# The first scan of a Mamba-2 layer and the MLP behind it: y in four PSUM banks, and copies, a mask, an identity fold and a mix in other places

## The chip, the cores and the metric

The kernel runs on one NeuronCore of a Trainium2 chip. The metric is device time in microseconds of one execution, as a median over runs. A profile is one execution recorded by the hardware profiler. PE is TensorE (matmuls), DVE is VectorE, ACT is ScalarE, POOL is GpSimd, and SP is the engine whose queue issues nearly all transfers. SBUF is the memory that all engines work on, and PSUM holds the results of matmuls in eight banks per partition.

## The reference

Two operations stand one behind the other. The first is a state space scan ("mamba2_ssd") over 4 batches of 8 heads, 768 positions, 32 features per head and 16 states, in chunks of 32:

```
for c in chunks:
    cum = cumsum(log a);  L = exp(cum_i - cum_j) where i >= j
    y[c]  = ((C B^T) * L) x  +  (C state) * exp(cum)
    state = exp(sum log a) * state + sum_j exp(cum_last - cum_j) * B_j x_j
```

Its y, as 3072 tokens of 256 features, goes into `h = y @ w_in` (256 to 2048), `g = h * sigmoid(1.702 h)` and `g @ w_out` (2048 to 256). The arguments x, a, B and C are of type float32. The two weights come as float64 and are turned to float32 on the chip.

## The kernel before, in words

**Tiling.** The 3072 tokens are cut into 6 groups of 512. A group is two pairs of 128-token chunks, and a chunk has two sides of 64 positions. The first group differs from the others in how its scan is made; its two pairs have the numbers 0 and 1. The order of the instructions on every engine is the order in which the program writes them down (`in_order` at the end), so whatever stands behind a waiting instruction on the same engine waits too.

**The first group.** Its steps are written out by hand at L1145 to L1193:

- `differ_of` and `decay_exp` (L551, L572) make the decays L of pairs 0 and 1, on PE and ACT.
- `mask_first(0)` (L645, on POOL) and `mask_blocks(1)` (L654, on ACT) make CT, which is C with the heads of a row group masked, for pairs 0 and 1.
- `fields(0)` and `rounded(0)` (L192, L195, L208, on DVE) begin the conversion of the first piece of w_in. `ends_first` (L465, DVE) makes Be.
- `score` (L677, PE) makes C B^T of both pairs in one PSUM area "cb" of four banks. `since_first` (L509 on PE, L514 on ACT) makes the decays since the start. `weigh` (L688, DVE) multiplies L by the scores, one instruction for each pair.
- Between the two weighings, `fetch(1, held=True)` writes one column of a buffer with a DVE memset (L171). The transfer of piece 1 of w_in waits for this memset, and with it everything behind it in SP's queue: pieces 2 to 5, and `rows_a`.
- `drops` (L519, DVE) copies the decays that carry a state on. `gain` (L708, PE) makes the increments of the states, `parts_first` (L727, ACT) masks them, `since_start` (L662, POOL) makes CsT, `clamp(0)` (L203, L204, ACT) goes on with the weights, and `keep_first` (L732 scan, then L737 copies on DVE and POOL) makes the states S.
- `fold_ident(1, nc.gpsimd)` (L332, POOL) makes the second half of a tile of identities, which `decay` needs from pair 3 on. `table(AF.Silu)` (L282, ACT) loads the table of Silu.
- `finish` makes y: `intra` (L814) and `inter` (L802) on PE, and two copies (L840, ACT) into yT. y lies in one PSUM area of four banks that takes the place of "cb", so its first matmul waits until the second `weigh` has read the scores. `dense(1)` (L1141) puts a matmul of ones on PE, whose result nobody reads.
- `join(0)` (L219, L225, DVE) ends piece 0 of w_in.

**The first group's MLP.** `hidden(0, f)` for f = 0 to 15 (L869 on PE, L873 Silu on ACT) needs w_in's pieces: piece 0 for f = 0, 1; piece 1 for 2, 3; piece 2 for 4, 5; piece 3 for 6, 7; piece 4 for 8 to 11; piece 5 for 12 to 15. `narrow(i)` converts piece i between these steps. Its order on DVE is `rounded(i)`, then `fields(i + 1)`, then `join(i)`. So the end of a piece stands behind the first look at the next one, which waits for that one's transfer. The ring of four PSUM banks "ff" holds h. `project_all(0)` (L967) follows, with the scan of the second group and the last pieces (8, 9) of the weights between its steps. Then come two steps `hidden(1, ...)`, the decay, scores and states of the third group, and from there on a form of Strassen's algorithm (`first`, L925 and L935; `product`, L1030; `mix`, L893 to L895), which has 7 products in the place of 8.

`mix_y(1)` (L893 to L895, DVE) makes the sums of yT that the second group's Strassen products need. It stands at place 15 of `project_all(0)`, ahead of `decay(n + 1)` (L399, then `ends`, L458), whose result the matmuls of `gain(later)` (L708) wait for.

Of the kernel before, what the change touches and what calls it, by code (L numbers as in the profile page):

```python
# [11 lines left out]
AF = mybir.ActivationFunctionType  # L12
# [4 lines left out]
P = 128  # L17
# [18 lines left out]
def kernel(  # L36
# [161 lines left out]
    def clamp(i):  # L198


        e = power[i]
        z = e.bitcast(FP32)
        nc.scalar.activation(z, e, AF.Relu, scale=-8.0, bias=edge[:, 0:1])  # L203
        nc.scalar.activation(e, z, AF.Relu, scale=-1.0, bias=edge[:, 1:2])  # L204

    def rounded(i):

        nc.vector.scalar_tensor_tensor(out=mantissa[i].bitcast(FP32), in0=bits[i][0],  # L208
                                       scalar=2.0 ** -32, in1=mantissa[i],
                                       op0=ALU.mult, op1=ALU.add)  # L210
# [21 lines left out]
    def narrow(i):  # L232
        rounded(i)
        if i + 1 < len(PIECES):
            fields(i + 1)
        join(i)
# [43 lines left out]
    def table(f):  # L280

        nc.scalar.activation(early, early, f)  # L282
# [47 lines left out]
    def fold_ident(k, engine=nc.vector):  # L330

        engine.tensor_tensor(  # L332
            out=idents[:, k * NH:(k + 1) * NH],
            in0=ident[:, :H].unsqueeze(1).to_broadcast([P, NH, H]),
            in1=ident[:, H:].unsqueeze(1).to_broadcast([P, NH, H]), op=ALU.add)
# [57 lines left out]
    yT = {}  # L393

    def decay(p):

        L = ssd.tile([P, 2 * NH * H], FP32, tag="L", name=f"L{p}", bufs=3)
        Ls[p] = L.rearrange("p (k r q i) -> p k r q i", k=2, r=R, q=Q)
        nc.vector.tensor_tensor_scan(  # L399
            out=L, data0=ra[p].rearrange("p k e -> p (k e)"),  # L400
            data1=idents.rearrange("p h i -> p (h i)"), initial=0.0, op0=ALU.mult, op1=ALU.add)
        for k in range(2):
            ends(p, k)
# [112 lines left out]

    def drops():

        nc.vector.tensor_copy(  # L519
            drop[:, :, 1:], since[0][:, :CG].rearrange("p c (s i) -> p (c s) i", s=2)[:, 1:, H - 1].unsqueeze(  # L520
                1).to_broadcast([P, Q * D, 2 * CG - 1]))

# [51 lines left out]
    def turn(p):  # L574
        turn_only(p)
        since_start(p)

    def bank(name):
        return ps.tile([P, 4 * P], FP32, tag="ff", name=name)

    def area(name):
        return psa.tile([P, R, 4 * P], FP32, tag="cb", name=name)
# [66 lines left out]
    def mask_blocks(p):  # L649

        s = st[p]
        s["CT"] = ssd.tile([P, 2, Q, P], FP32, tag="CT", name=f"CT{p}")
        for q in range(Q):
            nc.scalar.activation(s["CT"][:, :, q], s["tp"], AF.Copy, scale=part[:, q:q + 1])  # L654

    def since_start(p, engine=nc.vector):

        b, c = divmod(2 * p, NC)
        s = st[p]
        tp = s["tp"]  # L660
        s["CsT"] = ssd.tile([P, 2, P], FP32, tag="CsT", name=f"CsT{p}", bufs=3)
        engine.tensor_tensor(out=s["CsT"], in0=tp, in1=since[b][:, c:c + 2], op=ALU.mult)  # L662
# [66 lines left out]
    def keep_first():  # L729

        flat_steps = steps.rearrange("p e m -> p (e m)")
        nc.vector.tensor_tensor_scan(  # L732
            out=flat_steps, data0=drop.rearrange("p e m -> p (e m)"), data1=flat_steps,
            initial=0.0, op0=ALU.mult, op1=ALU.add)
        for p, copy in zip(range(PG), (nc.vector.tensor_copy, nc.gpsimd.tensor_copy)):
            state[p] = ssd.tile([P, 4, Q * D], FP32, tag="S", name=f"S{p}", bufs=3)
            copy(state[p], steps.rearrange("p e m -> p m e")[:, 4 * p:4 * p + 4])  # L737

# [36 lines left out]
    def finish(pairs, steps=range(2)):  # L775


        g, first = divmod(pairs[0], PG)
        early = pairs[0] < PG
        if 0 in steps:  # L780
            begun_y[pairs[0]] = area(f"y{pairs[0]}")[:, :, :len(pairs) * 2 * H].rearrange(
                "p (s t) (k i) -> p s t k i", s=2, i=H), set()
        both, begun = begun_y[pairs[0]]
        y = [both[:, i] for i in range(2)]

        def begin(i, t, parts):
            new = not begun & {(i, t, q) for q in parts}
            begun.update((i, t, q) for q in parts)
            return new

        def inter(n, p, sides=range(2)):

            for k in range(2):
                for i in sides:
                    m = 2 * k + i
                    if (4 * p + m) % (2 * NC) == 0:
                        continue
                    old = state[p][:, m - 1] if m else state[p - 1][:, 3]
                    for r in range(R):
                        t = r // 2  # L800
                        rows, to = slice(32 * r, 32 * r + 32), Q * D * (r % 2)
                        nc.tensor.matmul(  # L802
                            out=y[i][to:to + Q * D, t, 2 * n + k], lhsT=old[rows],
                            rhs=st[p]["CsT"][rows, k, SIDES[i]],
                            start=begin(i, t, range(Q * (r % 2), Q * (r % 2) + Q)), stop=early,
                            tile_position=(32 * r, to), skip_group_check=True)

        def intra(n, p):
            L = Ls[p]
            for k in range(2):  # L810
                for h in range(NH):
                    t, q = divmod(h, HB)
                    for i, side in enumerate(SIDES):
                        nc.tensor.matmul(  # L814
                            out=y[i][D * q:D * q + D, t, 2 * n + k], lhsT=rx[p][side, k, h],
                            rhs=L[side, k, h // Q, h % Q],
                            start=begin(i, t, (q,)), stop=not early, tile_position=(H * i, D * q),
                            skip_group_check=True)

        cols = slice(2 * first * P, 2 * (first + len(pairs)) * P)  # L820

        if first == 0:
            yT[g] = ffn.tile([P, NK, TG], FP32, tag="yT", name=f"yT{g}")
        if early:
            for n, p in enumerate(pairs):
                intra(n, p)
            dense(1)
            for i in range(2):
                for n, p in enumerate(pairs):
                    inter(n, p, (i,))  # L830
        else:
            for step in steps:
                for n, p in enumerate(pairs):
                    (inter, intra)[step](n, p)
            if 1 not in steps:
                return
        for i in range(2):
            o = yT[g][:, :, cols].rearrange("p t (k s i) -> p s t k i", s=2, i=H)
            if early:
                nc.scalar.activation(o[:, :, i], both[:, :, i], AF.Copy)  # L840
            else:
                nc.scalar.activation(o[:, i], y[i], AF.Copy)  # L842
        for p in pairs:
            state.pop(p - 1, None)
            st.pop(p)
            Ls.pop(p)
# [50 lines left out]
    def mix_y(g):  # L897
        mixed_y[g] = ffn.tile([P, 4, HT], FP32, tag="my", name=f"my{g}", bufs=1)
        mix(mixed_y[g], yT[g].rearrange("p k (t e) -> p k t e", t=2))
# [237 lines left out]
    def dense(n):  # L1137
        if n:
            t = bank("dense")
        for i in range(n):  # L1140
            nc.tensor.matmul(out=t[:, :4 * H], lhsT=ones,  # L1141
                             rhs=ones[:, :H].unsqueeze(1).to_broadcast([P, 4, H]),
                             start=True, stop=True, skip_group_check=True)
# [14 lines left out]
    mask_first(0)  # L1158
    for r in range(R):
        decay_exp(1, r, ab[1, r])  # L1160
    mask_blocks(1)
    turn_back()
    fields(0)
    ends_first(0)
# [13 lines left out]
        since_start(p, nc.gpsimd)  # L1178
    clamp(0)
    keep_first()  # L1180
    fold_ident(1, nc.gpsimd)
    table(AF.Silu)
    dense(1)
    finish(range(PG))
    dense(1)
    join(0)
    fields(1)
    clamp(1)
    rounded(1)
    fields(2)  # L1190
    clamp(2)
# [4 lines left out]
    def at(places, i, *work):  # L1196
        places.setdefault(i, []).extend(work)
# [13 lines left out]
    for i, k, c in ((2, 1, 1), (3, 2, 2), (4, 4, 4), (5, 6, 7), (6, 9, 12), (7, 12, 15)):  # L1211
# [2 lines left out]
    at(in_hidden[0], 9, lambda: spread(PG + 1), lambda: spread_rows(1))  # L1214
    n, p = 2 * PG, 3 * PG
    pairs = PG, PG + 1
    at(in_project[0], 0, lambda: turn(PG), lambda: narrow(8))
    at(in_project[0], 1, lambda: clamp(9))
    at(in_project[0], 2, lambda: decay(PG + 1), lambda: clip_rows(1),
       lambda: decay_rows(1), lambda: turn(PG + 1))  # L1220
# [4 lines left out]
    at(in_project[0], 15, lambda: finish(pairs, (1,)))  # L1225
    at(in_project[0], 13, lambda: mix_in(1), lambda: mix_in(2), lambda: mix_in(3),
       lambda: turn_blocks(2), lambda: decay(n))
    at(in_project[0], 15, lambda: mix_y(1))
    at(in_project[0], 6, lambda: spread(n), lambda: load(n), lambda: load_blocks(n + 1),
       lambda: load(n + 1, "b"), lambda: spread(n + 1))  # L1230
    at(in_project[0], 9, lambda: load(n + 1, "x"))
# [2 lines left out]
    after = {}  # L1234

    later = n, n + 1
    at(after, "H0", lambda: decay(n + 1), lambda: since_start(n),
       lambda: since_start(n + 1), lambda: gain(later), lambda: score(later),
       lambda: keep_both(later), lambda: weigh(n), lambda: weigh(n + 1))
    at(after, "H1", lambda: turn_out(0, 0), lambda: turn_out(0, 1))  # L1240
# [185 lines left out]
```

## Time and profile before

| what | value |
|---|---|
| median of 3 runs | 352.71 us (352.11 to 353.42) |
| the profiled execution | 351.27 us, span of its instructions 349.3 us |
| PE busy | 341.4 us (98%), 3388 instructions |
| DVE busy | 255.8 us (73%) |
| ACT busy | 149.2 us (43%) |
| POOL busy | 14.5 us (4%) |
| granted TensorE clock | 0.999 |
| transfers | 25.92 MB, mean 74 GB/s |

Matmuls are recorded as passes: one float32 matmul has two. In the timeline a row gives the start, the time from its first start to its last end, engine, line, operation, tiles and count; brackets hold the idle time of the engine ahead of it and what ended it. In the list of waits a row gives the total, the number of times and the longest. In the chain of waits a row gives the start, the time and what the end of the execution hung on.

### The profile page before, as it was taken

How to read it: one execution, taken by the hardware profiler on the slowest of the kernel's cores; microseconds unless marked ns; L12 is line 12 of the kernel's file. 1: busy time of each engine (PE TensorE's matmuls, PEld its weight loads, DVE VectorE, ACT ScalarE, POOL GpSimd, SP SyncE). 2: the span in 40 equal slices, each digit the busy share in tenths (PEclk: the TensorE clock that was granted, in tenths of full speed). 3: DMA queues.
4: the chain of work that ended last, by engine and by line, in shares of the span. 5: the costliest groups of instructions: out<-in, count | busy, mean ns of one | idle time of the engine just before them, and what ended most of it. 6: DMA issues, size and time to landing. Idle time of an engine off the chain costs nothing.

```text
span 349.3 us, 8110 instructions
## 1 busy us (share of the span) xinstructions
PE 341.4 (98%) x3388; PEld 272.9 (78%) x3388; DVE 255.8 (73%) x481; ACT 149.2 (43%) x332; POOL 14.5 (4%) x42
## 2 busy tenths in 40 slices
PE   7889999999999999999999999999999999999996
PEld 6634444547888888888888888888888888899996
DVE  5999998999679998739996558788464654455463
ACT  5778584005354322743442544432554331554320
POOL 8310000100000100000000000000000000000000
PEclk9999999999999999999999999999999999999999
DMA  6698998433626200445603026300000300000301
GB/s 163 149 324 179 242 217 189 84 84 69 116 39 145 47 0 6 73 81 108 116 21 56 2 70 123 66 0 3 0 4 2 60 2 1 0 2 0 62 0 61
DMA packets 89980, 25.92 MB, mean 74 GB/s; under 512 B 73432, under 2 KB 87128, under 8 KB 89944
## 3 DMA queue, kind: packets, MB, share of 16 engines
q1 hardware_dynamic: 89112, 24.88, 33.0%
q10 hardware_dynamic: 832, 0.52, 0.5%
q8 instruction: 26, 0.43, 0.5%
q14 instruction: 10, 0.08, 0.1%
HBM read 22.15 MB, written 3.24 MB: 73 GB/s over the span
## 4 chain that ended last, share of the span: by engine, by line
PE 75%; DMA 9%; DVE 8%; SPq 5%; issue 2%; ACT 0%; ACTq 0%; DVEq 0%
PE acc L1030 28%; PE X L925 19%; PE Y L935 14%; PE acc L1037 7%; DMA a<-scratch 4%; DMA bits<-in_moe_w_in_dram 3%; PE cb L677 2%; PE y L814 2%; SPq L180 2%; SPq L124 1%; DVE L L399 1%; PE y L802 1%; PE h L869 1%; DVE p L219 1%; SPq L150 1%
## 5 line engine op out<-in xcount | busy, mean ns | idle before, releaser
L930 ACT ACTIVATE ac<-X 128x256 f32<-128x256 f32 x76 | 29.1, 383 | 78.7 <-PE X L925 78.2
L1030 PE MATMUL acc<-mg,mw 128*128 128x256 f32 x192 | 54.5, 379 | 0.0
L902 ACT ACTIVATE gT<-gT 128x512 f32<-128x512 f32 (+1 forms) x76 | 39.3, 519 | 33.5 <-DVE gT L1057 32.8
L1057 DVE TENSOR_TENSOR gT<-Y,ac 128x512 f32<-128x512 f32 x38 | 26.2, 689 | 36.1 <-PE Y L935 30.4
L925 PE MATMUL X<-my,mi 128*128 128x256 f32 x152 | 45.1, 379 | 0.0
L1057 DVE TENSOR_TENSOR gT<-Y,b 128x256 f32<-128x256 f32 x38 | 15.9, 420 | 34.8 <-PE Y L935 34.8
L1030 PEld LDWEIGHTS acc<-mg,mw 128*128 128x128 f32 x192 | 36.5, 190 | 5.0
L869 PE MATMUL h<-yT,w_in 128*128 128x512 f32 (+2 forms) x108 | 35.6, 485 | 1.2 <-DVE w_in L225 1.2
L1030 PE MATMUL acc<-gT,w_out 128*128 128x256 f32 x128 | 35.5, 379 | 0.0
L869 PEld LDWEIGHTS h<-yT,w_in 128*128 128x128 f32 x108 | 18.2, 190 | 17.4 <-issue 13.6
L925 PEld LDWEIGHTS X<-my,mi 128*128 128x128 f32 x152 | 28.0, 190 | 3.7
L967 PE MATMUL o<-gT,w_out 128*128 128x512 f32 x64 | 28.6, 597 | 0.0
L893 DVE TENSOR_TENSOR mg<-gT 128x512 f32<-128x512 f32 x40 | 27.3, 682 | 0.0
L1030 PEld LDWEIGHTS acc<-gT,w_out 128*128 128x128 f32 x128 | 24.2, 190 | 3.4 <-ACT yT L842 0.2
L930 ACT ACTIVATE b<-X 128x256 f32<-128x256 f32 x38 | 14.6, 384 | 20.3 <-PE X L925 19.8
L925 PE MATMUL X<-yT,w_in 128*128 128x256 f32 x76 | 23.2, 389 | 0.0
L935 PE MATMUL Y<-my,mi 128*128 128x256 f32 x76 | 22.7, 381 | 0.1
L935 PE MATMUL Y<-yT,w_in 128*128 128x256 f32 x76 | 22.7, 381 | 0.0
L935 PE MATMUL Y<-yT,mi 128*128 128x256 f32 x76 | 22.5, 379 | 0.0
L925 PE MATMUL X<-my,w_in 128*128 128x256 f32 x76 | 22.5, 379 | 0.0
L967 PEld LDWEIGHTS o<-gT,w_out 128*128 128x128 f32 x64 | 11.8, 190 | 13.2 <-issue 12.6
L399 DVE TENSOR_TENSOR_SCAN L<-a,idents 128x1024 f32<-128x1024 f32 x9 | 20.5, 2279 | 0.1
(153 smaller groups left out, 543.4 us busy)
## 6 DMA issues: line engine op xcount, KB each, us to landing
a<-scratch SPq DMA_DIRECT2D x18, 256.0 KB, 5.1
bits<-in_moe_w_out_dram SPq DMA_DIRECT2D x8, 512.0 KB, 5.4
x<-in_x_dram SPq DMA_DIRECT2D x24, 128.0 KB, 3.4
out_dram<-ob SPq DMA_DIRECT2D x40, 64.0 KB, 1.9
bits<-in_moe_w_in_dram SPq DMA_DIRECT2D x8, 256.0 KB, 4.5
bits<-in_moe_w_in_dram SPq DMA_DIRECT2D x4, 512.0 KB, 10.9
b<-in_B_dram SPq DMA_DIRECT2D x20, 64.0 KB, 2.8
af<-in_a_dram SPq DMA_DIRECT2D x3, 384.0 KB
```

The costliest lines, as they stand in the source:

```text
L180: nc.sync.dma_start(out=dst[k], in_=src[k])
L399: nc.vector.tensor_tensor_scan(out=L, data0=ra[p].rearrange("p k e -> p (k e)"), data1=idents.rearrange("p h i -> p (h i)"), initial=0.0, ...
L869: nc.tensor.matmul(out=h[:, cols], lhsT=w_in[:, f, k], rhs=yT[g][:, k, cols], start=(k == 0 and e == 0), stop=(k == NK - 1), skip_group_ch ...
L893: nc.vector.tensor_tensor(out=t[:, 0:2], in0=B[:, :, 1], in1=B[:, 0], op=ALU.subtract)
L902: nc.scalar.activation(o, i, AF.Silu, scale=GELU_SCALE)
L925: nc.tensor.matmul(out=s["X"], lhsT=lhsT, rhs=rhs, start=i == "1", stop=i == "4", skip_group_check=True)
L930: nc.scalar.activation(copy, s["X"], AF.Copy)
L935: nc.tensor.matmul(out=o, lhsT=lhsT, rhs=rhs, start=s.pop("new", False), stop=i != "5", skip_group_check=True)
L967: nc.tensor.matmul(out=o[c], lhsT=w_out[:, c, f], rhs=gT[g, f // 2][:, f % 2], start=(f == 0), stop=(f == NF - 1), skip_group_check=True)
L1030: nc.tensor.matmul(out=acc[g][0][i][:, cols], lhsT=w, rhs=h[:, cols], start=(j == 0 and k == 0 and (i, 0) in begins), stop=(j == NF // 2 - ...
L1037: nc.tensor.matmul(out=o[k] if type(o) is list else o[:, cols], lhsT=h[:, cols], rhs=w, start=(j == 0 and (i, k) in begins), stop=(j == NF ...
L1057: nc.vector.tensor_tensor(out=o, in0=v, in1=w, op=ALU.add)
```

## The change

- y of the first group lies in four banks of the ring "ff" (one for each half of the tokens' features, t, and each side, i), and no longer in the area that held the scores. The matmuls of `inter` are put in order of t. After those of one t, two ACT copies of 128x256 evict its two banks. Before, two ACT copies of 128x512 followed after all of them.
- `drops` runs on ACT in the place of DVE. The second copy of `keep_first` runs on ACT in the place of POOL.
- The mask of pair 1 is one POOL operation (`mask_first(1)`) in the place of two ACT operations.
- `dense(1)` ahead of y becomes `dense(2)`; the two other dense matmuls, inside `finish` and behind it, are gone.
- `fold_ident(1)` goes from POOL to DVE, from ahead of y to place 0 of `project_all(0)`, between `rounded(8)` and `fields(9)`.
- `table(AF.Silu)` goes from ahead of y to behind `clamp(1)`.
- `mix_y(1)` goes from place 15 of `project_all(0)` to behind `decay(n + 1)`.

```diff
     def drops():
-        nc.vector.tensor_copy(
+        nc.scalar.copy(
             drop[:, :, 1:], ...
     def keep_first():
...
-        for p, copy in zip(range(PG), (nc.vector.tensor_copy, nc.gpsimd.tensor_copy)):
+        for p, copy in zip(range(PG), (nc.vector.tensor_copy, nc.scalar.copy)):
...
     def finish(pairs, steps=range(2)):
...
+            if early:
+                y = [bank(f"y0_{i}")[:, :2 * P].rearrange("p (k i) -> p k i", i=H) for i in range(4)]
+                begun_y[0] = [[y[2 * t + i] for t in range(NK)] for i in range(2)], set()
...
-            dense(1)
-            for i in range(2):
+            for t in range(NK):
                 for n, p in enumerate(pairs):
-                    inter(n, p, (i,))
+                    inter(n, p, (t,))
+                for i in range(2):
+                    nc.scalar.activation(
+                        yT[g][:, t, cols].rearrange("p (k s i) -> p s k i", s=2, i=H)[:, i], y[i][t],
+                        AF.Copy)
...
-    mask_blocks(1)
+    mask_first(1)
...
-    fold_ident(1, nc.gpsimd)
-    table(AF.Silu)
-    dense(1)
+    dense(2)
     finish(range(PG))
-    dense(1)
+    dense(0)
     join(0)
     fields(1)
     clamp(1)
+    table(AF.Silu)
     rounded(1)
...
-    at(in_project[0], 0, lambda: turn(PG), lambda: narrow(8))
+    at(in_project[0], 0, lambda: turn(PG), lambda: rounded(8), lambda: fold_ident(1),
+       lambda: fields(9), lambda: join(8))
...
-    at(in_project[0], 15, lambda: mix_y(1))
...
-    at(after, "H0", lambda: decay(n + 1), lambda: since_start(n),
+    at(after, "H0", lambda: decay(n + 1), lambda: mix_y(1), lambda: since_start(n),
```

More of the change, by code (lines that the diff above doesn't have):

```diff
@@ L780, in finish @@
         if 0 in steps:
[L781 to L784, printed above, removed]
+            if early:
+                y = [bank(f"y0_{i}")[:, :2 * P].rearrange("p (k i) -> p k i", i=H) for i in range(4)]
+                begun_y[0] = [[y[2 * t + i] for t in range(NK)] for i in range(2)], set()
+            else:
+                both = area(f"y{pairs[0]}")[:, :, :len(pairs) * 2 * H].rearrange(
+                    "p (s t) (k i) -> p s t k i", s=2, i=H)
+                begun_y[pairs[0]] = [[both[:, i, t] for t in range(NK)] for i in range(2)] + [both], set()
+        y, begun = begun_y[pairs[0]]
         def begin(i, t, parts):
@@ L789, in begin, with inter @@
             return new
-        def inter(n, p, sides=range(2)):
+        def inter(n, p, ts=range(2)):
             for k in range(2):
-                for i in sides:
+                for i in range(2):
                     m = 2 * k + i
@@ L800, in inter @@
                         t = r // 2
+                        if t not in ts:
+                            continue
                         rows, to = slice(32 * r, 32 * r + 32), Q * D * (r % 2)
                         nc.tensor.matmul(
-                            out=y[i][to:to + Q * D, t, 2 * n + k], lhsT=old[rows],
+                            out=y[i][t][to:to + Q * D, 2 * n + k], lhsT=old[rows],
                             rhs=st[p]["CsT"][rows, k, SIDES[i]],
@@ L814, in intra @@
                         nc.tensor.matmul(
-                            out=y[i][D * q:D * q + D, t, 2 * n + k], lhsT=rx[p][side, k, h],
+                            out=y[i][t][D * q:D * q + D, 2 * n + k], lhsT=rx[p][side, k, h],
                             rhs=L[side, k, h // Q, h % Q],
@@ L826, in finish @@
                 intra(n, p)
-            dense(1)
-            for i in range(2):
+            for t in range(NK):
                 for n, p in enumerate(pairs):
-                    inter(n, p, (i,))
+                    inter(n, p, (t,))
+                for i in range(2):
+                    nc.scalar.activation(
+                        yT[g][:, t, cols].rearrange("p (k s i) -> p s k i", s=2, i=H)[:, i], y[i][t],
+                        AF.Copy)
         else:
@@ L836, in finish @@
                 return
[L837 to L842, printed above, removed]
+            for i in range(2):
+                nc.scalar.activation(
+                    yT[g][:, :, cols].rearrange("p t (k s i) -> p s t k i", s=2, i=H)[:, i], y[2][:, i],
+                    AF.Copy)
         for p in pairs:
```

## The prediction

> **What bounds the kernel now.** I read the list of PE's waits first, since PE is busy for 98% of the span. PE waited seven times in all, and never after 86.2 us; these are the waits that the change comes near:
>
> ```profile
> PE y L814 <- DVE L L688: 1.2, 1, 1.2
> PE h L869 <- DVE w_in L225: 1.2, 2, 0.9
> PE A L708 <- DVE Be L458: 0.3, 1, 0.3
> PE y L802 <- DVE S L737: 0.3, 1, 0.3
> ```
>
> Behind 86.2 us a microsecond counts only if PE gets its work earlier or later. So what matters is when PE passes two points: the waits for w_in (0.88 us at 18.97 and 0.32 us at 33.26) and the 0.28 us at 86.20. PE's timeline shows the first two:
>
> ```profile
> 18.97 13.97 PE L869 MATMUL h<-yT,w_in 128*128 128x512 f32 x32 [0.88 <-DVE w_in L225]
> 33.26 3.67 PE L869 MATMUL h<-yT,w_in 128*128 128x512 f32 x8 [0.32 <-DVE w_in L225]
> ```
>
> The 32 passes are f = 0 to 7, 1.745 us each. At 33.26 f = 8 waits for w_in's piece 4. The chain of waits, read from 10 to 34 us, says what made that late:
>
> ```profile
> 10.61 0.71 PE cb L677 x32
> 11.34 1.24 DVE L L688 x2
> 12.60 0.37 SPq L180
> ...
> 18.29 11.01 DMA bits<-in_moe_w_in_dram
> ...
> 29.42 0.69 DVE p L192
> 30.11 0.60 DVE m L195
> 30.72 1.15 DVE p L219
> ```
>
> The reader sees a stream of transfers that starts at 12.60, as soon as the memset L171 (12.51) lets it, and whose last part, piece 5, lands at 29.30. DVE waits for it 0.30 us, and `join(4)` stands behind that look at piece 5: it ends at 33.12, and PE starts at 33.26. This time hangs on the **start of the stream**, not on y. The memset follows the first `weigh` (11.34), which waits for the second half of the scores.
>
> **The change, part by part.** Every sum is against the profiled execution: 351.27 us with a span of 349.3; the median of the runs shown is 352.71, so 1.44 us are added to come to it.
>
> *The head up to f = 0.* y no longer waits for the second `weigh` (1.2 us at 13.86), the drops leave DVE (0.69), the second state copy leaves POOL (0.86) and the fold leaves POOL. By itself: the second `weigh` ends at 13.71, scan 1.23, state copy 0.39, so S at 15.4 (before 16.09 and 16.59). `join(0)` takes 0.71 + 0.69 as L219 and L225 do at 20.81 and 21.55, and ends at 16.8 (before 18.82). `inter` of one t is half of 1.15, so t = 0 is done at 16.1. Two evictions of 128x256 take 0.66 (as the two of L514), so yT's first half stands at 16.85. f = 0 then begins near 17.0 in place of 18.97: **2 us earlier**. The ACT copies are not in the trace: the drops cost from 0.36 (ACT's 128x256) to 0.69 (DVE's own), the state copy from 0.36 to 0.86 (POOL's own); I take ACT's row for 512 elements, 0.58, and 0.4. The drops fit between the since rows (end 11.30) and the wait for A (12.04), and the state copy runs beside DVE's. The table load and its little activation (1.28 + 0.20) go behind `clamp(1)`. Behind them stand `clamp(2)` and the first Silu, which have over a microsecond. None of the moved steps issues a transfer, and SP's order is the same.
>
> But f = 2 needs piece 1, whose `join(1)` stands behind `fields(2)`, and piece 2's second half lands at 19.6 (issued at 14.31, 5.3 later). From that look to the end of `join(1)` took 2.1 us (20.14 to 22.24). So f = 2 begins at 21.8, not 20.5, and f = 8 would be wanted at 21.8 + 6 x 1.745 = 32.3. It still gets its weights at 33.1. **So the 2 us are worth nothing:** PE waits 1.3 us at f = 2 and 0.9 at f = 8. If that wait at f = 8 weren't there, the whole 2 us would be gained.
>
> *`mix_y(1)` behind `decay(n + 1)`.* The three mixes (82.01 to 83.53) leave the place ahead of the scan L399 (83.53) and L458, which end at 86.16. They would end at 84.8. PE gets there at 85.9, so the 0.28 us go. What is late next: `my` at 86.3, and PE reads it at 92.2. **-0.28 us.**
>
> *The fold on DVE* costs 0.68 (L332 at 3.13) at 54.2, where DVE idles 0.96 us for piece 9's transfer (55.19). Nothing; without that cover 0.68 on DVE, still off PE's path. *Dense:* one matmul fewer (0.70), in PE's idle time: nothing.
>
> *The mask of pair 1 on POOL* is the one that touches the stream. PE's rows end at 10.54, so the scores begin there in any case, if POOL is done. The risk lies with what runs beside it:
>
> ```profile
> 7.78 1.03 POOL L645 TENSOR_TENSOR CT<-Ct,part 128x512 f32<-128x512 f32 x1
> 8.50 0.59 DVE L192 TENSOR_SCALAR p<-bits 128x512 uint32<-128x512 uint32 x1 [0.22 <-DMA bits<-in_moe_w_in_dram]
> 9.02 0.41 DVE L195 TENSOR_SCALAR m<-bits 128x512 uint32<-128x512 uint32 x1
> 10.14 0.68 DVE L208 SCALAR_TENSOR_TENSOR m<-bits,m 128x512 f32<-128x512 uint32 x1
> 11.11 1.42 POOL L662 TENSOR_TENSOR CsT<-Ct,since 128x256 f32<-128x256 f32 x2 [2.30 <-ACT since L514]
> 15.73 0.86 POOL L737 COPY S<-steps 128x256 f32<-128x256 f32 x1 [3.21 <-DVE steps L732]
> 16.01 1.14 DVE L219 SCALAR_TENSOR_TENSOR p<-bits,p 128x512 uint32<-128x512 uint32 x1
> 16.56 1.71 POOL L332 TENSOR_TENSOR idents<-ident 128x512 f32<-128x512 f32 x1
> 17.18 1.64 DVE L225 SCALAR_TENSOR_TENSOR w_in<-m,p 128x512 f32<-128x512 f32 x1
> ```
>
> The last four rows show DVE and POOL taking turns. L219 ends 0.56 us after the POOL copy's end (16.59), the fold ends 1.12 after L219's end (17.15), L225 ends 0.55 after the fold's end (18.27); alone, L219 and L225 take 0.7. L192 too ends 0.28 after POOL's mask (8.81). So each seems to wait for the other's whole instruction, and the one that waited first goes first. With a second mask waiting from 8.81: L192 ends at 9.09 as before, the mask runs 1.03 to 1.12 and ends at 10.12 to 10.21 (in time for 10.54), L195 ends 0.28 later, at 10.40 to 10.49 in place of 9.43. Be (PSUM input) and the start of L208 follow at the spacing they have now (0.71 after L195's end), so L208 comes at 11.11 to 11.20. There it meets POOL's CsT, which comes at 11.11. If CsT is first, L208 waits for 0.71 (half of 1.42) until 11.82 and ends 0.55 later, at 12.4: the first `weigh` starts at 12.35 in place of 11.34, **1.0 us later**. If L208 is first, it ends at 11.8 and the delay is 0.45. If they take no such turns here, DVE has 0.52 us of idle time ahead of L688, and the delay is 0. A gain is excluded by PE's rows, which hold the scores at 10.54. I take 1.0, since the fold's row and the mask's own both put L208 behind CsT. The stream, f = 8 and all that PE does behind it shift by as much; so does the head, which stays about 1 us ahead.
>
> [...]
>
> Sum: +1.0 - 0.28 = **+0.7 us**: 352.0 for the profiled execution, 353.4 for the median.
>
> **The rivals.** (1) *L208 goes ahead of CsT:* +0.45 - 0.28 = +0.2, so 352.9. For it: the two come within 0.1 us. (2) *No delay of the stream:* -0.28, so 352.4. For it: DVE's 0.52 us of slack; against it: L219 and L225. (3) *The head's 2 us come through:* -2.0 - 0.28, so 350.4. That needs piece 5 to land 2 us earlier; nothing issues it earlier. Against it: the memset L171 stands behind the same `weigh` as before. (4) *Slower: TensorE's clock falls in the new waits.* The first matmuls (L437, 192 columns in 0.33 us each) ran at half the rate of L869 (512 in 0.44) for 3 us. PE's longest idle time so far, 1.2 us at 12.66, cost no such thing; the wait at f = 2 would be 1.3 and that at f = 8 1.0. If anything over 1.2 us brought the half rate back for 3.3 us behind f = 8, it would cost 1.65: +2.35, so 355.1. Against it: the granted clock is 9 in every slice.
>
> **How the numbers follow.** Chances: forecast 0.45, (1) 0.25, (2) 0.18, (3) 0.05, (4) 0.05, and 0.02 for others. The first three hold 0.88 and lie from 352.4 to 353.4. The three runs shown lie up to 0.7 us from their median, so the range is 352.0 to 354.1. What a measurement of this kernel can tell from no change is about 0.5%, 1.76 us. All three are within it: faster 0.05 (rival 3), same 0.89, slower 0.06 (rival 4 and 0.01).
>
> **What would show it.** Right: L195 beside a POOL mask taking over 1 us; the memset L171 at 13.5 (13.0 for rival 1, 12.5 for rival 2); f = 0 at about 18.0 and PE waits at f = 2 and f = 8 for DVE's w_in; f = 8 at 34.3 (33.7, 33.3); no wait of L708 for L458. Wrong: f = 8 before 33.0, or a new wait of PE behind 34 us.

## The result and the profile after

| what | before | after |
|---|---|---|
| median, first comparison (22 runs of each) | 352.17 us (350.9 to 354.01) | 351.82 us (350.39 to 353.46) |
| median, second comparison (29 and 12 runs) | 351.67 us | 350.55 us |
| the profiled execution, and its span | 351.27 us, 349.3 us | 352.58 us, 350.7 us |

The ratio of after to before is 0.9992 (95% interval 0.9977 to 1.0008) in the first comparison and 0.9964 (0.9947 to 0.998) in the second. The second interval lies below 1, the first does not. So the change is worth between nothing and half a per cent; by the prediction's bound of 0.5% it is **no change that can be told**. The prediction said this of the sign, with 0.89. Its time, 353.4 us, was 1.6 us too high, and 351.82 lies 0.18 us below its range. All ratios here are of fast executions; one slow execution each of e7 (714.64 us), e8 (360.61) and e9 (1460.66) is left out of them.

The profiled execution of after is one of its slower ones (352.58 against a median of 351.82), that of before one of its faster ones (351.27 against 352.17). The two traces must therefore not be set against each other by their spans. They were read wait by wait, and a second profile of after was taken (e9 below). First the waits of PE after, with the total, the number and the longest:

```profile
PE y L820 <- issue: 1.6, 2, 0.9
PE h L876 <- DVE w_in L225: 1.5, 1, 1.5
...
PE b L624 <- ACT L L572: 0.5, 1, 0.5
```

The wait of y for the second `weigh` (1.2) is gone, that of y for the states (0.3) and that of A for Be (0.3) too. The two waits for w_in (1.2 together) have become one of 1.5. New is a wait of y "for issue": no semaphore that the profile shows ended it. PE's timeline of after has both waits of that kind, and the one for w_in:

```profile
13.81 1.57 PE L820 MATMUL y<-L,x 64*32 64x64 f32 x95
16.05 0.48 PE L820 MATMUL y<-L,x 64*32 64x64 f32 x33 [0.67 <-issue]
16.45 1.67 PE L808 MATMUL y<-CsT,S 32*64 32x64 f32 x56
18.12 3.70 PE L876 MATMUL h<-yT,w_in 128*128 128x512 f32 x8
23.33 12.91 PE L876 MATMUL h<-yT,w_in 128*128 128x512 f32 x29 [1.51 <-DVE w_in L225]
...
79.17 1.10 PE L820 MATMUL y<-L,x 64*32 64x64 f32 x88
81.16 0.65 PE L820 MATMUL y<-L,x 64*32 64x64 f32 x40 [0.89 <-issue]
```

The 128 passes of one y fall apart in 95 + 33 and in 88 + 40, in the middle of a run in which nothing changes. f = 0 starts at 18.12 (18.97 before), f = 2 at 23.33, and f = 8 at 33.86 without a wait of its own (23.33 plus 6 x 1.745 makes 33.80).

The part on which the forecast turned, DVE and POOL around the second mask, in the timelines of these two engines:

```profile
7.93 2.03 POOL L645 TENSOR_TENSOR CT<-Ct,part 128x512 f32<-128x512 f32 x2
8.63 1.62 DVE L192 TENSOR_SCALAR p<-bits 128x512 uint32<-128x512 uint32 x1
10.17 0.42 DVE L195 TENSOR_SCALAR m<-bits 128x512 uint32<-128x512 uint32 x1
11.17 0.68 DVE L208 SCALAR_TENSOR_TENSOR m<-bits,m 128x512 f32<-128x512 uint32 x1
11.90 1.44 POOL L662 TENSOR_TENSOR CsT<-Ct,since 128x256 f32<-128x256 f32 x2 [1.94 <-ACT since L514]
12.14 2.36 DVE L688 TENSOR_TENSOR L<-L,cb 128x1024 f32<-128x1024 f32 x2 [0.30 <-PE cb L677]
13.31 0.06 DVE L171 MEMSET bits<- 128x1 uint32 x1
```

The two masks run back to back on POOL (7.93 to 9.96), and one L192 waits for both: it takes 1.62 us (0.59 before) and ends at 10.25, 0.29 us behind the second. DVE makes up the rest of it in its idle time: L208 ends at 11.85, and the first `weigh` still waits 0.30 us, for PE's scores. The memset comes at 13.31, near the forecast's 13.5, but for another reason: PE was late. Its matmuls at L551 began at 6.41 us, against 5.62 in the trace of before, and the row ahead of that, in PE's timelines of after and then of before, shows why:

```profile
4.57 1.91 PE L545 MATMUL ab<-below,identb 128*128 128x256 bf16 x8
```

```profile
4.31 1.04 PE L545 MATMUL ab<-below,identb 128*128 128x256 bf16 x8
```

The same eight matmuls took 1.91 us in one execution and 1.04 in the other. Nothing of the change stands ahead of them. The trace's own record of the granted clock tells the two apart: it begins with the full rate at 4.04 us in before and at 6.52 us in after, and the slow passes end near there.

### The profile page after: what moved, and what is told of

Same layout as the page of the kernel before. It is cut to its first block, busy times and chain, and to the rows that moved or that the text cites. A ratio compares the mean times of both kernels' runs of the same rounds, so it can differ in the third digit from the quotient of the medians.

```text
span 350.7 us, 8109 instructions
## 1 busy us (share of the span) xinstructions
PE 342.9 (98%) x3386; PEld 273.8 (78%) x3386; DVE 255.7 (73%) x481; ACT 149.9 (43%) x334; POOL 13.1 (4%) x41
## 4 chain that ended last, share of the span: by engine, by line
PE 94%; DVE 2%; DMA 2%; SPq 1%; issue 0%; ACT 0%; DVEq 0%
PE acc L1037 28%; PE X L932 19%; PE Y L942 14%; PE h L876 9%; PE o L974 8%; PE acc L1044 7%; PE y L820 2%; PE cb L677 2%; DMA bits<-in_moe_w_in_dram 2%; PE y L808 1%; PE A L708 1%; PE busy L437 1%; PE ab L551 1%; SPq L180 1%; PE ab L545 0%
## 5 line engine op out<-in xcount | busy, mean ns | idle before, releaser
L937 ACT ACTIVATE b<-X 128x256 f32<-128x256 f32 x38 | 14.6, 384 | 20.2 <-PE X L932 19.7
L974 PEld LDWEIGHTS o<-gT,w_out 128*128 128x128 f32 x64 | 11.8, 190 | 13.2 <-issue 12.8
```

Source lines behind the costliest of these rows:

```text
L937: nc.scalar.activation(copy, s["X"], AF.Copy)
L974: nc.tensor.matmul(out=o[c], lhsT=w_out[:, c, f], rhs=gT[g, f // 2][:, f % 2], start=(f == 0), stop=(f == NF - 1), skip_group_check=True)
```

## The experiments

The first eight were planned on two questions: whether the waits "for issue" come from the few PE instructions by which the change shifts y, and what each other part of the change is worth. The last four settle the size of the mask's cost and the nature of those waits. All of them compute the whole reference. Times are medians; each ratio is against the kernel before in the same comparison, with its 95% interval. It isn't the quotient of the two medians: in e5 they lie on opposite sides of no change.

| run | from | time us (before beside it) | ratio |
|---|---|---|---|
| e1_pad | after | 351.45 (351.47) | 0.9995 (0.9975 to 1.0014) |
| e2_before_less_dense | before | 351.75 (351.47) | 1.0001 (0.9979 to 1.0022) |
| e3_mask_on_act | after | 350.76 (351.47) | 0.9993 (0.9968 to 1.0017) |
| e4_stream_first | after | 350.77 (351.47) | 0.9983 (0.9965 to 1.0001) |
| e5_old_y | after | 351.54 (351.27) | 0.9981 (0.9962 to 1.0) |
| e6_before_stream_first | before | 351.02 (351.27) | 0.999 (0.9972 to 1.0008) |
| e7_pads | after | 358.42 (351.27) | 1.0176 (1.0138 to 1.0214) |
| e8_together | after | 358.19 (351.27) | 1.0167 (1.0127 to 1.0207) |
| e9_after_again | after | 350.55 (351.67) | 0.9964 (0.9947 to 0.998) |
| e10_before_mask_alone | before | 351.78 (351.67) | 1.0007 (0.9983 to 1.0032) |
| e11_pads17 | after | 354.8 (351.67) | 1.0097 (1.006 to 1.0135) |
| e12_mask_and_stream | after | 350.41 (351.67) | 0.9973 (0.9952 to 0.9994) |

**e1_pad.** After, with one small matmul more ahead of the scan (two passes), so that everything behind the first y stands on PE where it stood before the change (the first y itself stands four passes further on than before, two of them by the second dense matmul).

```diff
-            pads(0, busy)
+            pads(1, busy)
```

> The changed kernel with one tiny matmul more (32x32, two passes, 4 instructions on PE) ahead of the masks, so that all of PE's later instructions stand 4 places further on in its instruction stream, about as in the kernel before. Theory 1 (instructions): in the profile of the changed kernel PE stops twice inside a run of small matmuls of y with nothing to wait for but 'issue' (0.67 us at 16.05, 0.89 us at 81.16), because the next block of its instructions was asked for too late; one dense matmul less moved the place at which it is asked for. Then the stall at 81 goes and the time falls by 0.9 to 1.2 us. Theory 2 (the stalls are an accident of the one execution): no change, within 0.3 us, and stalls of this kind stand in this profile too.

The wait in the second group's y stays, 0.72 us at 80.95, one of 0.23 us stands in the first y, and the time is that of before. So the few instructions that the change takes away aren't the cause.

**e2_before_less_dense.** Before, without the dense matmul ahead of y, so that all behind the first y is shifted as in after.

```diff
     table(AF.Silu)
-    dense(1)
     finish(range(PG))
```

> The kernel before without the one dense matmul ahead of y (4 instructions on PE fewer). Theory 1 (instructions): a stall 'issue' of about 0.9 us appears in the second group's y (near 80 us), and the time rises by 0.9 to 1.2 us. Theory 2 (accident): same time within 0.3 us, no such stall; the dense matmul lies in PE's idle time.

A wait appears (0.42 us at 81.33), smaller than after's. Together with e1 the picture was unclear: the waits come with the shift and without it.

**e3_mask_on_act.** After, with the mask of pair 1 back on ACT.

```diff
-    mask_first(1)
+    mask_blocks(1)
```

> The changed kernel with the mask of pair 1 back on ACT. Theory A (turns of DVE and POOL): L192 takes about 0.6 us in the place of 1.62, the first weighing and the memset that lets the stream go come earlier by up to 0.5 us (less if PE's scores are late in that execution), and the time falls by 0.3 to 0.5 us. Theory B (the scores on PE set the memset in any case): memset at the end of the scores plus 1.3 us as now, same time within 0.2 us.

L192 takes 0.43 us again, but the memset comes at 13.23, 1.28 us behind the end of the scores (11.95). With the mask on POOL it was 1.28 behind them too (12.03 and 13.31). So the mask's place costs the stream nothing in these executions. No y wait for issue is in this profile, though the program stands on PE as after's does.

**e4_stream_first.** After, with the memset, the fetches of pieces 1 to 5 and `rows_a` ahead of the scores.

```diff
-    score(range(PG), since_first)
-    weigh(0)
     fetch(1, held=True)
...
     rows_a(az, (nc.sync,))
+    score(range(PG), since_first)
+    weigh(0)
     weigh(1)
```

> The changed kernel with the memset and the transfers of pieces 1 to 5 and of a put ahead of the scores and of both weighings, so that the stream starts about 1.3 us earlier (near 12.0 by the last profile, or when DVE is through with rounded(0)). Theory S (the stream's start sets f = 2 and f = 8): PE's wait at f = 2 falls from 1.5 us to near 0 and the time falls by 1.2 to 1.5 us. Theory H (what the scan's first half takes on PE, DVE and ACT sets them): no gain, within 0.3 us. If the transfers of x and of the first blocks are disturbed by the stream, the time rises.

The memset comes at 11.76, and the wait at f = 2 goes. But y now waits 1.31 us, at the same 95th pass as in after. PE's timeline of this run:

```profile
14.01 1.54 PE L820 MATMUL y<-L,x 64*32 64x64 f32 x95
16.86 0.48 PE L820 MATMUL y<-L,x 64*32 64x64 f32 x33 [1.31 <-issue]
```

f = 0 starts at 18.94 and f = 8 at 33.27. What the earlier stream gives, the longer wait takes.

**e5_old_y.** After, with the old `finish`: y in the area of the scores, evicted at its end, and three single dense matmuls. It keeps the moved copies, mask, fold and mix.

> The changed kernel with y as it was: one PSUM area that waits for the second weighing, evicted by sides at the end, and the three single dense matmuls. All other edits stay. Theory S (the stream of w_in's pieces decides): f = 0 starts some 0.5 to 1.5 us later than in the changed kernel (18.1), and f = 2 and f = 8 stand where they stood against the memset L171 (10.0 and 20.5 us behind it), so the time is the same within 0.3 us. Theory Y (the four banks bring what the change brings): 0.5 to 1.5 us slower.

f = 0 comes 6.45 us behind the end of the scores; before it is 7.74, after 6.09, and in e9 5.85. So the copies, the fold and the table load made some 1.3 us of the head, and the halves of y some 0.5. f = 8 waits 1.52 us for w_in and starts at 33.63.

**e6_before_stream_first.** The edit of e4, made in before.

> The kernel before with the memset and the transfers of pieces 1 to 5 ahead of the scores and weighings. Theory S: before, f = 8 waited only 0.32 us for the stream, and f = 0 waits for join(0), which the stream does not touch, so the gain is 0.3 us at most, against up to 1 us for the same edit in the changed kernel. Theory H (the stream's start matters by itself): the same gain as in the changed kernel with this edit.

Again the memset is early (11.54), and again y waits for issue, here behind its 97th pass, for 1.20 us at 16.97. The waits belong to no version.

**e7_pads** and **e8_together.** After with 24 small matmuls and 2 dense ones at the start in the place of 5 dense ones, which moves all that follows by 42 passes; e8 has the edits of e3 and e4 as well.

```diff
-    keep_busy(5, 0)
+    keep_busy(2, 24)
```

> The changed kernel with 24 tiny matmuls in the place of three of the five first dense ones: PE is as busy there for about as long, but all later PE instructions stand 84 places further on in its instruction stream, and so the places where a new block of instructions is asked for and where it is needed. Theory I (PE stalls named 'issue' are waits for a block of instructions that was asked for behind a burst of transfers): no stall in the first y (it was 0.67 us) and none in the second group's y near 81 us (0.42 to 0.89 in three of six profiles), since the blocks are asked for about 84 instructions earlier in the same work; time 0 to 1 us less. Theory N (accident): stalls of this kind at the same places again, same time.

> The changed kernel with the stream first, the mask of pair 1 on ACT, and the 24 tiny matmuls. Theory S and I: f = 0 at about 17.5, no wait or a short one at f = 2, f = 8 at 32 to 32.5 in the place of 33.3 to 33.9, and no 'issue' stall at 81 us; time 0.8 to 1.5 us less than the changed kernel. If the stream was not what decided, the same time within 0.3 us.

Both lost 7 us, which no theory had foreseen. The list of PE's waits in e7, and its timeline:

```profile
PE y L820 <- issue: 3.6, 3, 1.7
PE y L808 <- issue: 3.3, 1, 3.3
```

```profile
13.61 0.98 PE L820 MATMUL y<-L,x 64*32 64x64 f32 x53
15.16 0.99 PE L820 MATMUL y<-L,x 64*32 64x64 f32 x75 [0.56 <-issue]
16.08 1.56 PE L808 MATMUL y<-CsT,S 32*64 32x64 f32 x52
20.98 0.47 PE L808 MATMUL y<-CsT,S 32*64 32x64 f32 x4 [3.34 <-issue]
```

The waits sum to 7.0 us (0.56, 3.34, 1.71 and 1.35), 5.4 more than after's waits for issue. With 2.3 us of half clock rate (below), 1.5 less at f = 2 and 0.4 less ahead of L551, that makes 5.8, and the spans of the two profiles differ by 5.7. The places explain the waits: counted from the start of the program they stand behind passes 349, 476, 2382 and 2892. After's and e1's stand behind 349 and 854, those of e4, e6, e9 and e12 behind 349, those of e2 and e10 in the second group behind 855. The count is the same whatever stands there, y's 53rd pass or its 95th. The distances are 127 (476 less 349), 505 (about 4 x 126), 1906 (about 15 x 127) and 510 (4 x 127.5). A pass has two PE instructions, a weight load and a matmul (the page of after counts 3386 of each), so there is such a place at every 256 instructions, a few semaphore instructions among them. The page's list of queues has one for instructions, and the transfers of e7 between 18.5 and 19.7 us have one entry of it; columns are packets, MB and the time they took as a share of 16 engines:

```profile
q1 hardware_dynamic: 364, 0.35, 90.9%
q8 instruction: 1, 0.02, 4.6%
```

That one block is on record from 18.69 to 19.57 us, beside 0.35 MB of w_in, and PE goes on at 20.98, 1.41 us behind its end. In every wait of this kind in these profiles the block's transfer ends 1.1 to 1.5 us before PE goes on (after: 14.67 and 16.05, 79.87 and 81.16; e4: 15.62 and 16.86). Where no data is moved, a block's transfer mostly begins 0.5 to 1.4 us after PE has passed the place before it, some 127 passes earlier; behind the stream of w_in it began from 1.7 us (after) to 6.0 us (e12) after that, 3.1 in e9 and 3.5 in e7. So if a block is asked for when PE passes the place before, which the traces don't show directly, it takes about 3 us from request to use (2.8 to 3.7 where PE waited and no data was in front), and more when transfers are in front (5.8 in e7, from 15.16 to 20.98). The 127 passes of y need 1.5 us, and so PE runs dry in them. This also tells when the wait at 81 us comes. Its block began at 78.68 to 79.03 us in the four profiles that waited there (after, e1, e2, e10) and at 76.1 to 77.2 in before, e3 to e6, e9 and e12, which did not.

The page of after has 26 transfers of that queue with 0.43 MB in all, 16 KB each, for the 3386 passes, one for 130 on the average. At the places inside the large matmuls no wait shows: the lists of PE's waits (before, after, e1 to e7, e9 to e12) have waits for issue with y alone, where one cost from 0.2 us (e1) to, in the timeline of e8, 4.0 us.

The long wait of e7 had a second price. The windows of e7, with PE's busy time, count, granted clock, the DMA share and GB/s:

```profile
20.00:21.00 1.00, 0.01 (x2) 0.50 0.95 270
...
24.00:25.00 1.00, 1.00 (x3) 0.50 1.09 385
25.00:26.00 1.00, 1.00 (x3) 0.56 1.11 397
26.00:27.00 1.00, 1.00 (x4) 1.00 1.12 330
```

The clock was granted at 0.50 after a pause of 3.34 us, and the passes of h came every 0.85 us in the place of 0.43 until 25.8, which cost some 2.3 us. By the trace's record the clock fell at 19.06, when the pause, begun at 17.64, was 1.42 us old, and rose at 25.89. The pauses of 1.51 us in after and 1.83 us in e2 did not do this, so the length of a pause alone doesn't tell whether the clock falls.

**e9_after_again.** The changed kernel itself, for a second profile.

> The changed kernel as it is, once more, for a second profile. Theory (waits for PE's instruction blocks come and go from execution to execution): the two waits of y without a releaser (0.67 us at 16.05, 0.89 at 81.16) come out with other sizes, each between 0 and 1.3, and a fast execution ends the span at 348.5 to 349.5 in place of 350.7. Rival (they belong to the changed order of the program): both come back within 0.2 us of their size and the span is 350.5 or more. Either way DVE's mask of piece 1's pair (L192 at 8.6) takes 1.6 us behind both POOL masks. Time 351.0 to 352.0.

The wait at 16.05 is 0.42 here, that at 81.16 is not there, and the span is 348.6: same program, 2.1 us less. PE's waits and the start of the stream on DVE:

```profile
PE busy L437 <- DVE ones L296: 1.2, 1, 1.2
PE h L876 <- DVE w_in L225: 0.7, 1, 0.7
PE b L624 <- ACT L L572: 0.5, 1, 0.5
PE y L820 <- issue: 0.4, 1, 0.4
```

```profile
8.52 1.55 DVE L192 TENSOR_SCALAR p<-bits 128x512 uint32<-128x512 uint32 x1 [0.24 <-DMA bits<-in_moe_w_in_dram]
...
12.22 2.36 DVE L688 TENSOR_TENSOR L<-L,cb 128x1024 f32<-128x1024 f32 x2 [0.52 <-PE cb L677]
13.39 0.06 DVE L171 MEMSET bits<- 128x1 uint32 x1
```

**e10_before_mask_alone.** Before with nothing but the mask of pair 1 on POOL (the edit of e3, the other way).

> The kernel before with only the mask of pair 1 moved to POOL. The prediction's step: the first weigh and the memset come 1.0 us later than the scores allow, and the time rises by 1.0. What the profile of the changed kernel says instead: both POOL masks run back to back, L192 takes 1.6, L208 ends at 11.8 to 11.9, and the first weigh starts there or at the end of the scores, whichever is later: with scores that end at 11.2 to 11.3 a delay of 0.5 us, with scores that end at 12.0 none. Time +0.0 to +0.5. Rival (the mask is dear, and something else in the change paid it back): +1.0 or more.

```profile
7.73 2.03 POOL L645 TENSOR_TENSOR CT<-Ct,part 128x512 f32<-128x512 f32 x2
...
8.79 1.25 DVE L192 TENSOR_SCALAR p<-bits 128x512 uint32<-128x512 uint32 x1 [0.29 <-DMA bits<-in_moe_w_in_dram]
10.97 0.68 DVE L208 SCALAR_TENSOR_TENSOR m<-bits,m 128x512 f32<-128x512 uint32 x1
12.16 2.36 DVE L688 TENSOR_TENSOR L<-L,cb 128x1024 f32<-128x1024 f32 x2 [0.52 <-PE cb L677]
```

These are rows of POOL's and DVE's timelines. L208 ends at 11.65, and DVE idles 0.52 us for the scores, as much as in before. The time is 0.1 us above before; its interval, -0.6 to +1.1 us, would not by itself exclude the forecast's 1.0, but the profile lacks the delay on which that 1.0 rests.

**e11_pads17.** The edit of e7 with 17 small matmuls in the place of 24, so that all stands 14 passes (28 PE instructions) earlier than in e7.

```diff
-    keep_busy(5, 0)
+    keep_busy(2, 17)
```

> As the kernel with 2 dense and 24 small matmuls at the start (358.42), but with 17 small ones: all later matmuls stand 14 x 2 places earlier in PE's program. Theory (the waits sit at fixed places of PE's program, one every 127 or so matmuls, where the next 16 KB block is asked for when the one before is entered; a block that is used up in under about 5 us while transfers run makes PE wait): the place that fell on y's 52nd state matmul (3.34 us at 20.98) falls on the 10th pass pair of the projection behind it and is not waited for, the one at 211.5 (1.71) falls behind y and goes too, the half-rate passes from 21.4 to 25.8 go with the long wait; the waits at 15 and at 260 to 266 stay (0.5 and 1.1). Time 351.5 to 353.0. Rival (the first matmuls must be dense, or TensorE's clock is lost at 20 to 26 us): 358 again, half rate again.

The waits of e7 at 15.16, 20.98 and 211.5 are gone (the first since PE was slow ahead of it, see below), and that in the last group's y, again behind pass 2892, stays with 1.47 us at 263.4. The theory of the blocks had said this of the last three places; it had expected the wait at 15 to stay. The time missed both theories: 354.8 in the place of 351.5 to 353.0, or 358. PE's timeline shows why:

```profile
5.71 1.16 PE L551 MATMUL ab<-cum,pick 32*64 32x128 f32 x32 [0.48 <-DVE part L387]
...
263.42 0.34 PE L820 MATMUL y<-L,x 64*32 64x64 f32 x14 [1.47 <-issue]
```

The 32 passes of L551 take 1.16 us; in after they take 0.70. All of PE is that slow up to some 17.8 us, the scores end at 15.18, and f = 8 starts at 36.20, 2.3 us behind after's. So the rival had a point, at another place: with 2 dense and 17 small matmuls at the start, TensorE's rate stayed low for 12 us behind the start of L551 (5.71) in e11. The windows of the profile give a granted clock of 1.00 for these slices, but that is no reading: the trace's record of the clock begins with the full rate at 17.36 us in e11, at 5.41 in e7 and at 6.52 in after, and has nothing ahead of it. In e7 the three changes of the record (5.41, 19.06, 25.89) lie four and two times 3.41 us apart (13.65 and 6.83), and the full rate of before and of after lasts 344.75 us, 101 times 3.41. In e7 the first matmuls of 128 rows and columns (2.00 to 5.35) fill nearly the whole 3.41 us ahead of the grant. In e11 they run from 1.88 to 5.23, and steps of 3.41 us, counted back from 17.36, put a boundary at 3.70, in their midst; behind them come smaller ones (32*64 and 32*128 in the rows). That this decided between e7, with 7 small matmuls more, and e11 is an estimate, and no run tests it. Why the rate then stayed low while PE was busy for 11.1 of the 12 us from 4 to 16 (the sum of e11's windows) was not shown.

**e12_mask_and_stream.** After with the edits of e3 and e4, the version that the single runs pointed to.

> The changed kernel with the mask of pair 1 on ACT as before, and with the fetches of pieces 1 to 5 ahead of the scores: the two that each came out at 350.8. Theory: the stream begins at about 11.7 and the waits for w_in at f = 2 and f = 8 go (0.24 at most); y waits for its block (about 1.3 us near 16.5), since the block's transfer now stands behind the stream, so f = 0 starts at 18.7 to 19.0 and f = 8 at 32.8 to 33.3. Time 350.3 to 350.9, at most 0.4% below the kernel before. Rival (the head's 2 us come through once the stream is early): f = 0 at 17.5, f = 8 at 31.5, 349.3.

350.41 us, 0.9973 (0.9952 to 0.9994). y waits 0.85 us for issue, f = 0 starts at 18.26 and f = 8 at 32.64, after a wait of 0.29. It can't be told from after itself (350.55 in the same comparison).

## Why the prediction was right in sign and too high in size

The forecast was 352.71 + 1.0 - 0.28. Term by term:

- **The base.** Three runs of before gave a median of 352.71; 22 runs gave 352.17, and the later comparisons 351.47, 351.27 and 351.67. This is 0.54 us of the miss, and by itself enough to bring the time into the range. The range itself was uneven: 0.7 us above the forecast, but only 0.4 below rival 2's 352.4. With 0.7 on both sides it would have begun at 351.7, and 351.82 would lie in it.
- **The mask on POOL, +1.0: the step that failed.** The step was "L192 ends at 9.09 as before, the mask runs 1.03 to 1.12 ..., L195 ends 0.28 later", with L208 then behind CsT. The waiting DVE instruction did not get its turn between the two masks: it waited for both. L192 took 1.25 to 1.73 us in the seven profiles with this mask on POOL (1.62, 1.55 and 1.25 in after, e9 and e10) and 0.43 to 0.68 in the seven with it on ACT. L208 then went ahead of CsT, which waits for PE's rows and came at 11.90 in after. The first `weigh` began 0.1 us behind the end of the scores, as in before, in six of the seven. In e7, whose scores ended at 11.67, L208 ended at 12.02, and the delay was 0.27: there the mask cost 0.16 us. By the ends of L208 in after, e9 and e10 (11.65 to 11.85) the price would be 0.3 to 0.5 us in an execution whose scores end at 11.23, as in the trace that the forecast was read from; that is an estimate. In the profiles of the other runs, e11 apart, they end from 11.63 to 12.45. So the step also failed in taking a slack from one execution, the one with the earliest PE of them all. In the rows of after, e9 and e10 the second mask, the next in POOL's queue, went ahead of the L192 that waited already, and L192 ended 0.28 or 0.29 us behind it.
- **The head, "the 2 us are worth nothing": half right.** f = 0 came nearer to the scores by 1.65 to 1.9 us, as worked out. The wait at f = 2 came too (1.3 said; 1.51, 0.71, 1.06 and 0.72 in after, e9, e3 and e1). But the wait of 0.9 at f = 8 did not: there was 0.13 in e1 and none in the other three. From the memset to f = 8 it took 20.74, 20.78, 20.43 and 20.72 us with the old y (before, e2, e10, e5) and 20.54, 19.65, 19.81 and 19.52 with the new one (after, e1, e3, e9): on the mean 0.8 us less. f = 8 came at 32.91 in e9, ahead of the 33.0 that the prediction names as a sign of being wrong. The step held that piece 5 lands 16.7 us after the stream's start whatever happens. It landed 16.78, 16.82, 16.46 and 16.76 us after the memset in the four profiles with the old y, and f = 8 began 3.96 or 3.97 us after that in each. With the new y it landed after 16.06, 15.65, 15.83 and 15.21 us. There f = 8 began 12.8 to 13.0 us after piece 2 had landed. The passes from f = 2 on fill this stretch on PE, and the conversions fill it on DVE, and in after and e9 piece 5 lay there 0.6 and 0.5 us before DVE looked at it. So the gain is that of transfers that landed sooner, and what then holds f = 8 is piece 2 and the work behind it. Why they landed sooner was not shown, nor that the new y did it: with the stream first, piece 5 took 15.71 us with the old y (e6) and 15.73 and 16.99 with the new one (e4, e12).
- **mix_y, -0.28: too large.** The wait of L708 for Be is in one of four profiles with the old place (before; not e2, e6, e10) and in none with the new one. On the mean that is 0.07 us. Other waits of the same line, for CsT, came in e1 (0.93 us at 65.63) and e12 (0.53 at 65.25).
- **The rivals.** What happened is rival 2's mechanism (the stream isn't delayed by the mask) with a part of rival 3's gain. Rival 1's order, L208 ahead of CsT, came too, and cost nothing but in e7.
- **The clock (rival 4).** After has a wait of 1.51 us at f = 2, with the granted clock at 9 in every slice. In e7 the clock did fall, within a pause of 3.34 us, which cost some 2.3 us. In e2 a pause of 1.83 us passed without it.
- **Not thought of: the instruction blocks.** e7, e8 and e11 apart, they add from 0 to 1.6 us to the profiled executions, 1.56 us to that of after and nothing to that of before. The prediction's list of PE's waits, which has eight of them and not seven, has none of this kind.

With the terms as measured, 352.17 + 0 - 0.8 - 0.07 gives 351.3. The first comparison gave 351.82; by their ratios the two comparisons put after 0.3 and 1.3 us below before. What the halves of y are worth alone stays open: e5, without them, can't be told from after by its time.

## What to carry to other kernels

A gap of half a microsecond that is read from one execution is no slack of the kernel: look which engine was early in that execution, and lay the forecast out for the later one as well. Where an instruction takes longer beside another engine's, as L192 beside POOL's masks here (0.59 us beside one, 1.62 beside two), count the whole queue of the one against the waiting instruction of the other. And look for a wait without a releaser in a run of small matmuls: here it stood at a fixed count of instructions (places about 127 passes apart), it was longer where the stream of transfers began earlier (0.67 and 0.42 us in after and e9, 1.31, 1.20 and 0.85 in e4, e6 and e12), and moving the program by 84 PE instructions cost 7 us here (e7), moving it by 4 nothing that can be told (e1).

## What the runs showed of the hardware that was not expected

- PE's waits for issue stand at places about 127 passes (256 instructions) apart, with a 16 KB transfer of instructions ahead of each. From passing a place to the next block's use took about 3 us in quiet stretches and 5.8 us behind the stream of w_in (15.16 to 20.98 in e7).
- In a pause of PE of 3.34 us the granted clock was halved, 1.42 us after its start, and the passes were slow for 4.9 us behind it (e7); pauses of 1.51 us (after) and 1.83 us (e2) did not do this.
- The drops on ACT took 1.03 us (12.13 in after), above both ends of the bounds that the prediction had for them, 0.36 and 0.69. The state copy took 0.67 (15.69 in after), where 0.4 was taken.
- Between executions whose first matmuls are the same, the start of L551 varied by 0.8 us (5.62 to 6.41), and with it the scores, the stream and f = 0. The full clock rate was granted at 4.04 us in the earliest of them (before) and at 6.3 to 7.4 in after, e2, e4, e6, e9, e10 and e12, which started L551 at 6.39 or later.
